# Soft-cap attention and a gated convolution FFN: float64 weights fetched once, six tiles of q and k fetched by rows, a new order

## The chip, the cores and the metric

The kernel runs on one core of a Trainium2 chip. The metric is the device time in microseconds (us) of one execution. Before the change three runs gave 723.64, 722.81 and 723.58 us, the median is 723.58 us. One of them, 723.64 us, was profiled; the rows below come from it. Its span, from the first to the last instruction of the program, is 721.9 us, so 1.7 us lie around it.

## What is computed

Inputs: q, k, v of shape (8 batches, 12 heads, 448, 64) in float32, a cap of 30, and three float64 weights: w_val and w_out (768 x 768) and conv_w (5 x 768).

```python
scores = scale * q @ k.T                      # per batch and head, scale = 1/8
scores = cap * tanh(scores / cap)
attn = exp(scores - max); attn = attn / (sum(attn) + 1e-9)
x = attn @ v                                  # heads side by side: (8, 448, 768)
gate = sigmoid(causal depthwise conv of x with conv_w, 5 taps)
out = (gate * (x @ w_val)) @ w_out            # float32
```

## The kernel before

**Units.** Two heads are one pair, so there are 48 pairs, six for each batch (a block). A pair is held transposed, 128 partitions (2 heads x 64) by 448 positions. Per pair the steps are: load q, k and v; turn q and k (`turn`, L471, VectorE 32x32 block transposes of tiles that `load_blocks` fetched with four DMAs each, in runs of 32 floats); `scores` in four chunks (L501 for three of them, L492 for the last 64 keys); `tanh` and `exp` on ScalarE (L512, L516); `attnv` and `sums` on TensorE (L551); `swap`, a GpSimd memset on which the other half of these products waits (L588); the row sums turned, inverted, moved by four small GpSimd copies (L617, L618) and spread (L623); `mul`; and then the split of x in two float32r parts and five taps of the convolution. `dup` is a GpSimd copy inside the v tile (L769). The first 13 pairs use plain float32 score products, the others three float32r products.

**FFN.** Per block, `val` multiplies x by w_val and `out_part` the gated product by w_out, each in quarters of 18 matmuls (L692). The second quarter of a `val` needs the last three pairs of its block.

**Weights.** [...] `wsteps` cuts the two matrices in twelve parts of 128 x 2 x 384. For each part two DMAs brought the same 768 KB: `weight_load` into `w_raw` as 32-bit words, and `late_load` into `w_late`, placed two bytes further so that the 32 bits in the middle of each float64 are one word. `float64_split` has three steps: first on ScalarE (two passes over the high words, the second in place), second and third on VectorE (2 and 3 instructions). Each scratch tile has one buffer (`RB = 1`).

**Order.** All engines run the order that is written out in three tables, `PAIRS`, `BLOCKS` and `WEIGHTS`: each number is the place of one step, and the steps are issued in ascending order. The engines' queues are in order; SyncE (SP) issues every DMA, so a DMA that waits for a buffer holds those behind it. The numbers are only an order, not times.

**Start.** q and k of pair 0 are loaded before the branch on the cap, into the tiles `u2` that later hold x.

Of the kernel before, what the change touches and what calls it, by code (L numbers as in the profile page):

```python
# [21 lines left out]
P = 128  # L22
# [11 lines left out]
RB = 1  # L34
# [8 lines left out]
    "load_q load_k load_v dup tq tk q_hi k_hi q_lo k_lo scores scores scores scores tanh tanh tanh tanh exp exp exp exp "  # L43
# [4 lines left out]
- - -36.4291 -24.374 -37.9619 -37.5136 - - - - -29.0953 -27.9246 -34.5266 -32.3914 -28.5027 -27.2632 -34.3824 -29.2176  # L48
  -24.6849 -25.7265 -31.13 -28.7197 - - -23.292 -23.2461 -22.7205 -21.0767 -20.9932 -19.802 -18.4009 -17.5513 -17.1655
  -16.0407 -15.7774 -15.7173 -15.1748 -15.0823 -15.0278 -14.5506 -14.1049 -13.877 -13.7921 -12.1034 -11.3551 -8.4558  # L50
  -6.415 -6.392 -6.1725 -5.1224 -4.4352
-37.4386 -37.4387 -35.491 -16.4956 -31.9763 -33.561 - - - - -26.9758 -18.0782 -24.612 -27.4284 -25.6836 -16.3335
  -20.2913 -26.1892 -19.7974 -15.283 -18.6445 -15.7935 - - -14.7101 -13.2839 -12.8874 -12.572 -12.3419 -12.2373
  -12.0247 -11.7255 -10.2241 -9.8171 -9.7551 -9.4464 -9.3257 -9.2797 -8.9784 -8.7292 -8.7165 -8.6069 -8.4916 -7.3936
  -6.0864 -2.8949 -7.1359 -6.0411 -5.329 -5.0552 -3.5349
-37.0301 -36.7637 -10.1568 -8.8454 -19.4908 -17.8612 - - - - -13.7951 -13.7224 -17.7339 -17.092 -13.4291 -11.281
  -13.9097 -14.3472 -9.6416 -10.6643 -11.4185 -12.0276 - - -8.6127 -8.6004 -8.5032 -8.4243 -7.5194 -7.2147 -7.1119
  -6.8708 -6.8368 -6.5822 -6.5821 -6.5008 -6.4379 -6.4378 -6.3814 -6.0863 -5.9744 -5.2517 -4.9229 -4.7084 -3.3457
  -1.1639 -3.9739 -3.7703 -3.5511 -3.4556 -2.9168
# [24 lines left out]
-4.1741 -4.3642 -2.2358 -1.7665 -3.1083 -3.6244 - - - - -2.4685 -1.9312 -1.1375 -2.4014 -2.105 -1.6867 -1.0432 -1.8568
  -1.4142 -1.3686 -0.8526 -0.9598 - - -0.8636 -0.8069 -0.7143 -0.6844 -0.625 -0.5659 -0.4845 -0.4512 -0.3601 -0.326
  -0.251 -0.2504 -0.2414 -0.2063 -0.1205 0.0278 0.3998 0.4886 0.6433 0.7081 1.404 2.5253 1.1579 2.1234 2.7966 2.9888
  3.8991
-5.9312 -3.3656 -1.1405 -0.5559 -2.9017 -2.683 - - - - -0.7716 -1.9644 -1.3399 -1.8509 -0.7511 -1.8327 -1.0977 -1.1584
  -0.5037 -1.3997 -0.0772 -0.0242 0.0805 - -0.0596 0.0005 0.0501 0.0712 0.1653 0.0882 - 0.2485 0.3584 0.4957 0.4993
  0.5303 0.5444 0.5665 - 0.8974 1.0769 1.3554 1.5395 1.561 1.8421 1.9775 2.8868 3.0021 3.8177 3.9114 4.0692  # L90
-2.8216 -3.1447 -1.1298 -0.8483 -2.5982 -1.8133 - - - - -1.2603 -1.5752 -1.3468 -0.9904 -0.6953 -1.5612 -1.0722
  -0.5119 0.4867 0.1382 0.1363 -0.4553 0.7181 - 0.6129 0.6573 0.6654 0.6655 1.0809 0.7518 - 1.081 1.2749 1.4957 1.4958
  1.4959 1.496 1.4961 - 1.6372 1.7452 1.7801 1.8906 1.9143 2.3235 2.5502 2.0327 2.81 3.2719 3.4628 3.5498
-2.2014 -2.8734 -1.1244 1.0266 -1.7634 -1.6803 - - - - -1.5271 -0.8689 -1.1528 0.239 -0.9106 -0.3824 -0.5713 0.388
  1.2563 0.737 1.0745 0.4539 1.6006 - 1.538 1.5604 1.5605 1.5828 1.6328 1.6241 - 1.6329 1.7747 1.9622 1.9713 1.9796
# [146 lines left out]
"""  # L242

WEIGHTS = """
-36.4388 -34.2302 -17.3317 -15.7359 -7.9977
-7.2769 -4.5437 -3.4181 -3.2841 -2.5607
-2.0227 -1.1687 -1.5194 -1.2043 0.239
-0.0716 1.368 1.0934 1.5723 2.0259
# [35 lines left out]
def shifted(t, n):  # L284


    return t.bitcast(I32)[..., 1:2 * n:2]
# [696 lines left out]
```

## Time and profile before

| | |
|---|---|
| median of the runs | 723.58 us |
| the profiled execution | 723.64 us, span 721.9 us |
| TensorE busy | 682.3 us (95%) |
| ScalarE busy | 546.8 us (76%) |
| VectorE busy | 518.9 us (72%) |
| GpSimd busy | 96.5 us (13%) |
| DMA moved | 65.02 MB, 90 GB/s over the span |

PE is TensorE's matmuls, PEld its weight loads, ACT ScalarE, DVE VectorE, POOL GpSimd, SPq the issuing of DMAs. In 40 equal slices of the span (18 us each; a digit is the busy share in tenths) the page shows:

```
PE   4877899799999999999999999999999999999996
DVE  1588798688387676987877966867788785877520
ACT  5888899597787887977877869786989877985311
DMA  6689898866142242325333441225151343110002
```

The chain of work that ended last is 73% TensorE.

### The profile page before, as it was taken

What the parts mean: (1) busy time and instruction counts of PE and PEld (TensorE: products, weight loads), DVE (VectorE), ACT (ScalarE), POOL (GpSimd) and SP (SyncE); (2) the same over time, 40 slices, a digit from 0 to 9 for tenths busy, and PEclk for the clock granted to TensorE, in tenths of its full rate; (3) what the DMA queues carried; (4) which work ended last, traced back from release to release, by engine and by line L of the source; (5) the groups of instructions that cost most, each with busy time, mean ns of one, the idle gap of its engine ahead of it and who ended that gap; (6) DMA issues with size and microseconds to landing.
All of it is one profiled execution on the core that took longest, in us unless ns stands there. A gap on an engine that the chain in (4) does not pass through costs nothing.

```text
span 721.9 us, 30880 instructions
## 1 busy us (share of the span) xinstructions
PE 682.3 (95%) x13714; PEld 577.4 (80%) x13714; DVE 518.9 (72%) x928; ACT 546.8 (76%) x740; POOL 96.5 (13%) x356
## 2 busy tenths in 40 slices
PE   4877899799999999999999999999999999999996
PEld 1554687579989898888888988897888898898995
DVE  1588798688387676987877966867788785877520
ACT  5888899597887787877977869786989877985311
POOL 0111102021002011011102111112111101121000
PEclk9999999899999999999999999999999999999999
DMA  6689898866142242325333441225151343110002
GB/s 125 118 181 205 200 245 181 211 153 117 33 77 63 61 79 54 64 70 104 75 54 67 85 83 33 63 61 115 29 94 36 79 104 56 38 50 25 24 2 92
DMA packets 242284, 65.02 MB, mean 90 GB/s; under 512 B 228832, under 2 KB 236000, under 8 KB 242144
## 3 DMA queue, kind: packets, MB, share of 16 engines
q1 hardware_dynamic: 242144, 62.99, 40.4%
q8 instruction: 109, 1.79, 1.1%
q14 instruction: 31, 0.25, 0.1%
HBM read 51.94 MB, written 11.01 MB: 87 GB/s over the span
## 4 chain that ended last, share of the span: by engine, by line
PE 73%; ACT 3%; DVE 2%; SPq 2%; issue 2%; POOL 0%; DMA 0%; DVEq 0%; POOLq 0%; ACTq 0%
PE psf L692 40%; PE psa L551 19%; PE pss L501 9%; PE pss L692 3%; PE pss L492 2%; SPq L347 1%; ACT pt L512 1%; ACT pt L516 1%; ACT L516 1%; SPq L360 1%; DVE gate L662 0%; ACT g_h L723 0%; DVE g_l L408 0%; DMA vn<-in_v_dram 0%; ACT ph L516 0%
## 5 line engine op out<-in xcount | busy, mean ns | idle before, releaser
L512 ACT ACTIVATE pt<-pss,rc 128x896 f32<-128x896 f32 x144 | 142.8, 1004 | 69.1 <-PE pss L501 67.8
L692 PE MATMUL psf<-wo,g_h 64*128 64x384 f32 x1248 | 163.3, 338 | 1.7 <-POOL token L700 1.6
L692 PE MATMUL psf<-xh,wv 64*128 64x448 f32 x1104 | 161.5, 369 | 1.3 <-ACT xh L646 0.6
L516 ACT ACTIVATE pt<-pt,capt 128x896 f32<-128x896 f32 x144 | 147.0, 1042 | 1.0
L551 PE MATMUL psa<-pt,vn 64*32 64x224 f32 x4416 | 132.3, 355 | 6.7 <-issue 3.5
L662 DVE SCALAR_TENSOR_TENSOR gate<-u,cw,gate 128x448 f32<-128x448 f32 x192 | 126.1, 664 | 2.1 <-ACT gate L658 0.8
L551 PEld LDWEIGHTS psa<-pt,vn 64*32 64x32 f32 x4416 | 80.4, 106 | 51.0 <-issue 23.0
L692 PEld LDWEIGHTS psf<-wo,g_h 64*128 64x128 f32 x1248 | 112.4, 184 | 9.7 <-issue 4.2
L692 PEld LDWEIGHTS psf<-xh,wv 64*128 64x128 f32 x1104 | 103.1, 184 | 15.0 <-issue 3.5
L692 PE MATMUL psf<-wo,g_l 64*128 64x384 f32 x624 | 105.3, 332 | 0.2 <-DVE g_l L408 0.2
L692 PE MATMUL psf<-xl,wv 64*128 64x448 f32 x552 | 102.1, 363 | 0.0
L692 PEld LDWEIGHTS psf<-wo,g_l 64*128 64x128 f32 x624 | 58.9, 184 | 0.6 <-DVE g_l L408 0.5
L692 PEld LDWEIGHTS psf<-xl,wv 64*128 64x128 f32 x552 | 52.6, 184 | 4.7 <-DVE xl L408 0.4
L602 DVE STREAM_TRANSPOSE zt<-psa 128x256 f32<-128x256 f32 x46 | 20.4, 444 | 48.6 <-PE psa L551 48.4
L501 PE MATMUL pss<-qt,kt 64*128 64x448 f32 x156 | 41.4, 622 | 12.1 <-DVE guard L417 8.0
L720 DVE TENSOR_TENSOR gate<-psf,gate 128x448 f32<-128x448 f32 x46 | 27.3, 616 | 34.3 <-PE psf L692 33.2
L623 DVE STREAM_TRANSPOSE zt<-rc 128x512 f32<-128x512 f32 x48 | 34.0, 707 | 24.8 <-POOL rc L618 24.5
L617 POOL COPY rc<-rc 32x8 f32<-32x8 f32 x96 | 34.9, 364 | 122.9 <-DVE rc L610 119.9
L523 DVE TENSOR_TENSOR pa<-pt 128x896 f32<-128x896 f32 x38 | 41.0, 1080 | 13.9 <-ACT pt L516 13.9
L751 ACT COPY osb<-psf 128x384 f32<-128x384 f32 x52 | 23.7, 477 | 32.6 <-PE psf L692 29.8
L723 ACT CAST g_h<-gate 128x448 fp32r<-128x448 f32 x48 | 25.9, 561 | 19.2 <-DVE gate L720 19.2
L501 PE MATMUL pss<-qh,kh 64*128 64x448 f32 x210 | 40.2, 380 | 0.0
(97 smaller groups left out, 1075.4 us busy)
## 6 DMA issues: line engine op xcount, KB each, us to landing
out_dram<-osb SPq DMA_DIRECT2D x56, 192.0 KB, 2.3
kn<-in_k_dram SPq DMA_DIRECT2D x188, 56.0 KB, 2.6
qn<-in_q_dram SPq DMA_DIRECT2D x188, 56.0 KB, 2.7
vn<-in_v_dram SPq DMA_DIRECT2D x96, 96.0 KB, 2.8
w_raw<-in_moe_w_val_dram SPq DMA_DIRECT2D x6, 768.0 KB, 5.4
w_late<-in_moe_w_val_dram SPq DMA_DIRECT2D x6, 768.0 KB, 5.3
w_raw<-in_moe_w_out_dram SPq DMA_DIRECT2D x6, 768.0 KB, 4.9
w_late<-in_moe_w_out_dram SPq DMA_DIRECT2D x6, 768.0 KB, 6.1
```

The costliest lines, as they stand in the source:

```text
L501: nc.tensor.matmul(ps[:, j, :S], st[x][r, c], st[y][r], start=(n == 0), stop=(n == len(parts) - 1))
L512: nc.scalar.activation(st["p", i], st.pop(("s", i)), AF.Tanh, scale=rc8)
L516: nc.scalar.activation(t, t, AF.Exp, scale=capt)
L523: nc.vector.tensor_tensor(st["a"], st["a"] if i else st["p", 0], st["p", i + 1], op=ALU.add)
L551: mm = nc.tensor.matmul(bank(p, h)[o, cols], left, right, start=start, stop=(st["left"][kind] == 0), skip_group_check=True)
L617: nc.gpsimd.tensor_copy(rc[GROUPS[g], 1], rc[GROUPS[g + 1], 1])
L623: nc.vector.transpose(st["zt"][:, :4 * ZQ].rearrange("p (c e) -> p c e", e=BLK), rc)
L662: nc.vector.scalar_tensor_tensor(g, u[:, i:i + S], cw[:, hp, i:i + 1], g, ALU.mult, ALU.add)
L692: mm = nc.tensor.matmul(outs[k], left[r], right[r], start=(swap == 0 and first), stop=(swap == 1 and last))
L720: nc.vector.tensor_tensor(g, psums.pop((b, d))[:, :S], g, op=ALU.mult)
L723: nc.scalar.copy(gated["h"][:, d, TL:], gates[b * NPAIR + d])
L751: nc.scalar.copy(osb, psums.pop((b, "o", m))[:, :NH])
```

## The change

- `weight_load` fetches a part with two DMAs of 128 rows. `late_load` is gone; `low_words` takes its place: a GpSimd copy of the two middle 16-bit words of each float64, 128 x 1536 elements, out of `w_raw`. It reads what the in-place pass of step one overwrites, so that ScalarE pass has to come after it.
- q and k of pairs 0, 1 and 2 (`TURNED = 3`) are fetched by `load_rows`: two DMAs a tile, four rows of 64 floats to a partition. `turns` makes eight TensorE transposes against an identity into one `pss` tile of PSUM, and `tq`, `tk` copy out of PSUM on VectorE. The io tiles and `u2` grow from 448 to 512 columns; GpSimd builds the identity before the branch.
- The three tables are new, with one more step, `turns`. The number of steps of every other kind is as before.

```diff
+def load_rows(nc, t, src, p):
+    _, H, S, D = src.shape
+    b, hp = divmod(p, H // 2)
+    t = t[:CH, :2 * S * D // CH].rearrange("r (n j d) -> r n j d", j=2, d=D)
+    for j in range(2):
+        nc.sync.dma_start(t[:, :, j], src[b, 2 * hp + j].rearrange("(r n) d -> r n d", r=CH))
...
             raw = wsc.tile([P, WC, NH, 2], I32, name="w_raw", bufs=RB)
-            rows = w[c.start * P:c.stop * P, nh * NH:(nh + 1) * NH].bitcast(I32)
-            nc.sync.dma_start(raw.rearrange("p i n t -> p i (n t)"), rows.rearrange("(i p) n -> p i n", p=P))
+            for i in range(WC):
+                r = (c.start + i) * P
+                nc.sync.dma_start(raw[:, i], words(w[r:r + P, nh * NH:(nh + 1) * NH]))
             wstate[n] = raw
-        def late_load(n):
-            w, c, nh, _ = wsteps[n]
-            late = wsc.tile([P, WC, 4 * NH + 2], U16, name="w_late", bufs=RB)
-            rows = w[c.start * P:c.stop * P, nh * NH:(nh + 1) * NH].bitcast(U16)
-            nc.sync.dma_start(late[:, :, 1:1 + 4 * NH], rows.rearrange("(i p) n -> p i n", p=P))
-            wlate[n] = shifted(late, NH)
+        def low_words(n):
+            wlate[n] = wsc.tile([P, WC, NH], I32, name="w_late", bufs=RB)
+            nc.gpsimd.tensor_copy(wlate[n].bitcast(U16).rearrange("p i (n k) -> p i n k", k=2), wstate[n].bitcast(U16)[..., 1:3])
...
+        def turns(p):
+            ps = ps_s.tile([P, 2, 512], F32, name="pss")
+            for x, name in enumerate("qk"):
+                t = loads.pop((name, p))[:CH, :2 * S * D // CH].rearrange("r (n e) -> r n e", e=2 * D)
+                for n in range(S // CH):
+                    nc.tensor.matmul(
+                        ps[:, x, n * CH:(n + 1) * CH], t[:, n], ident[:CH, :CH], start=True, stop=True, is_transpose=True
+                    )
+                loads[name, p] = ps[:, x, :S].rearrange("p (n r) -> p r n", r=CH)
...
-            nc.vector.transpose(t, loads.pop((name, p)))
+            src = loads.pop((name, p))
+            if p < TURNED:
+                nc.vector.tensor_copy(t.rearrange("p (r n) -> p r n", r=CH), src)
+            else:
+                nc.vector.transpose(t, src[:, :S])
```

The first steps of the new order, by queue. SP: k2, weight part 0, k1, q1, the five DMAs of conv_w, v0, v1, q2, part 1, q3. TensorE: `turns` 0, three chunks of scores 0, `turns` 1, the last chunk of scores 0, three chunks of scores 1, `turns` 2, one chunk of scores 1, and then `attnv` 0. ScalarE: two `tanh` of pair 0, step one of weight part 0, a third `tanh`. GpSimd: `low_words` 0, `dup` 0, the small copy of conv_w, `dup` 1, `low_words` 1, `swap` 0. `low_words` is the instruction just ahead of step one, with no other ScalarE step between them, for parts 1, 6, 8, 9 and 11; for part 8 `weight_load`, too, has no ScalarE step between it and step one.

## Rows read from the trace of the kernel before

**Rows 1.** Windows: length, busy us (count) of each engine, clock, DMA share, GB/s

```profile
0.00:180.00 180.00, 151.89 (x3562) 108.53 (x3564) 131.02 (x244) 143.18 (x186) 24.59 (x91) 0.97 0.79 174
180.00:660.00 480.00, 475.50 (x9454) 417.47 (x9452) 367.25 (x649) 390.53 (x530) 69.69 (x253) 1.00 0.32 66
```

**Rows 2.** Waits of TensorE, 0 to 180 us: us in total, times, longest

```profile
PE psa L551 <- issue: 9.7, 6, 3.6
PE pss L501 <- DVE guard L417: 8.0, 1, 8.0
PE pss L492 <- DVE qt L471: 3.1, 2, 1.8
PE pss L501 <- DVE qt L471: 2.7, 3, 1.6
...
PE pss L501 <- issue: 1.0, 1, 1.0
```

**Rows 3.** Windows in which the granted clock (third last column) is lowest

```profile
66.00:72.00 6.00, 4.65 (x56) 2.05 (x64) 5.52 (x11) 4.23 (x7) 1.75 (x5) 0.72 0.72 163
...
131.00:136.00 5.00, 2.03 (x21) 0.89 (x21) 3.63 (x6) 2.12 (x4) 0.09 (x1) 0.66 0.79 141
136.00:144.00 8.00, 8.00 (x140) 5.97 (x140) 3.90 (x9) 3.52 (x5) 0.00 (x0) 0.79 0.86 207
```

**Rows 4.** DMA queues, 130 to 134 us: packets, MB, share of 16 engines

```profile
q1 hardware_dynamic: 2712, 0.59, 84.0%
q8 instruction: 1, 0.02, 2.3%
```

**Rows 5.** DMA issues of the whole span: count, KB each, us to landing

```profile
vn<-in_v_dram SPq DMA_DIRECT2D x96, 96.0 KB, 2.8
...
w_late<-in_moe_w_val_dram SPq DMA_DIRECT2D x6, 768.0 KB, 5.3
```

**Rows 6.** Timeline, 0 to 40 us: start, us, engine, line, operation, count

```profile
6.29 0.40 SPq L439 DMA_DIRECT2D w_raw<-in_moe_w_val_dram  x1
6.74 2.03 SPq L347 DMA_DIRECT2D kn<-in_k_dram  x4
...
11.98 1.01 SPq L360 DMA_DIRECT2D vn<-in_v_dram  x2
13.04 0.73 SPq L361 DMA_DIRECT2D vn<-in_v_dram  x1
...
15.56 0.28 POOL L769 COPY vn<-vn 64x128 f32<-64x128 f32 x1 [10.88 <-DMA vn<-in_v_dram]
...
17.66 1.36 PE L551 MATMUL psa<-pt,vn 64*32 64x224 f32 x48
...
28.72 4.17 SPq L321 DMA_DIRECT2D cw_raw<-in_moe_conv_w_dram  x5
```

**Rows 7.** Timeline, two groups of score matmuls

```profile
15.22 0.61 PE L492 MATMUL pss<-qt,kt 64*32 64x224 f32 x16 [1.36 <-DVE qt L471]
...
20.25 1.02 PE L501 MATMUL pss<-qt,kt 64*128 64x448 f32 x4
```

**Rows 8.** Groups of GpSimd by form: busy us, mean ns, idle before

```profile
L730 POOL TENSOR_SCALAR g_l<-g_l 128x384 fp32r<-128x384 f32 x4 | 2.1, 517 | 1.1 <-DVE g_l L408 1.1
L332 POOL COPY cw_m<-cw_raw 128x60 uint16<-128x60 uint16 x1 | 0.2, 234 | 0.4 <-DMA cw_raw<-in_moe_conv_w_dram 0.4
```

**Rows 9.** Groups of ScalarE by form: busy us, mean ns, idle before

```profile
L668 ACT ACT_TABLE_LOAD x24 | 30.8, 1283 | 0.4
L516 ACT ACT_TABLE_LOAD x23 | 29.5, 1283 | 0.4
...
L300 ACT ACTIVATE w_t<-w_raw 128x768 f32<-128x768 f32 x12 | 11.2, 930 | 1.3 <-DMA w_raw<-in_moe_w_val_dram 0.8 <-DMA w_raw<-in_moe_w_out_dram 0.4
```

**Rows 10.** Timeline around 67 us, VectorE and GpSimd

```profile
66.77 0.18 POOL L617 COPY rc<-rc 32x8 f32<-32x8 f32 x1 [6.21 <-DVE rc L610]
...
67.13 0.58 DVE L408 TENSOR_TENSOR xl<-u,xh 128x448 fp32r<-128x448 f32 x1
67.21 0.55 POOL L617 COPY rc<-rc 32x8 f32<-32x8 f32 x1
```

More of the change, by code (lines that the diff above doesn't have):

```diff
@@ L42 @@
 STEPS = (
-    "load_q load_k load_v dup tq tk q_hi k_hi q_lo k_lo scores scores scores scores tanh tanh tanh tanh exp exp exp exp "
+    "load_q load_k load_v dup turns tq tk q_hi k_hi q_lo k_lo scores scores scores scores tanh tanh tanh tanh exp exp exp exp "
     "add add av av av av sums sums sums sums swap av2 av2 av2 sums2 sums2 sums2 turn_sums recip shift spread mul x_hi x_lo "
@@ new lines @@
+-1.6385 -1.509 -0.1777 0.4865 - -1.6291 -0.6406 - - - - -0.1059 -0.097 0.2865 -0.4254 -0.0041 0.2299 0.5879 -0.3546
+  0.426 0.6017 0.8286 0.8243 - - 0.5078 0.8301 0.9701 0.9702 0.9778 0.9853 1.0253 1.0254 1.1146 1.2279 1.2441 1.3341
+  1.3469 1.3547 1.3909 1.5049 1.5403 1.6201 1.6989 1.7485 2.2673 2.779 2.2192 2.2767 2.2925 2.8204 3.001
+-1.4478 -2.3682 -0.3329 0.5078 - -0.7352 -1.5218 - - - - -0.2547 0.0436 0.057 -0.7006 -0.0982 0.1447 0.3254 -0.0033
+  0.139 0.3565 0.4943 0.5181 - - 0.5762 0.5918 0.6327 0.6414 0.6424 0.6427 0.6686 0.6864 0.6878 0.6884 0.7016 0.7123
+  0.7609 0.9603 1.0221 1.0507 1.0548 1.0989 1.1532 1.1907 2.4555 2.7151 1.4661 2.1357 2.6827 2.933 3.2721
@@ new lines @@
+-1.9115 -2.3483 -0.4141 0.1687 - -0.9563 -1.247 - - - - -0.5341 -0.3823 -0.6029 -0.2015 -0.467 -0.2625 -0.5988 -0.0495
+  -0.2595 0.225 -0.3864 0.2693 - - 0.2757 0.3613 0.3614 0.3615 0.37 0.3701 0.3702 0.3703 0.3935 0.5559 0.556 0.5561
+  0.5992 0.5993 0.5994 0.7161 0.7227 0.7912 1.0268 1.1106 1.9171 2.0192 2.6796 2.9152 2.9406 3.308 3.6016
+-2.2442 -2.5286 -0.5356 -0.5032 - -1.0558 -1.0112 - - - - -0.2888 -0.9159 -0.9622 -0.5875 -0.2095 -0.6062 -0.6227
+  -0.4479 0.0235 -0.2877 -0.2616 -0.2523 - - 0.1587 0.2193 0.2448 0.3779 0.4141 0.5449 0.5788 0.6313 0.639 0.7798
+  0.8115 0.8503 0.8707 0.9729 1.0244 1.0812 1.2195 1.2816 1.3721 1.4335 2.3975 2.5699 1.9494 2.0746 2.2294 3.0315
+  3.1536
@@ new lines @@
+-2.2399 -2.6359 -0.3985 0.67 - -1.227 -0.9804 - - - - -0.8382 -0.029 -0.4885 -0.1912 -0.5516 0.1465 -0.3818 -0.0337
+  0.4745 0.6233 0.4855 0.7528 - - 0.7112 0.9214 0.9277 0.9278 0.9279 0.928 0.9281 0.9282 0.9519 0.9734 0.9735 0.9736
+  0.9737 0.9738 0.9739 1.5419 1.8331 1.8986 1.9946 2.137 2.3625 3.246 2.2122 2.6622 2.7042 3.9978 4.0246
+-2.4046 -1.6476 -0.2473 0.0748 - -0.6617 -1.4629 - - - - -0.2957 -0.5245 0.581 -0.0208 -0.2043 -0.2113 0.6768 0.522
+  0.673 0.2651 1.0378 1.0412 0.8707 - 1.2008 1.2579 1.258 1.2581 1.2583 1.2582 - 1.2584 1.321 1.4874 1.541 1.5839
+  1.584 1.5841 - 1.8854 2.0212 2.0354 2.0355 2.1637 3.5808 3.7577 3.0036 3.072 3.6717 3.8646 4.6128
@@ new lines @@
+-1.2232 -1.4429 1.3692 1.6624 - -0.6145 -0.4235 - - - - 0.1261 -0.2635 -0.0965 0.3196 0.3216 0.013 0.0246 0.5137
+  1.2984 0.5106 0.8566 1.2744 1.6058 - 1.8324 1.8325 1.8326 1.8327 1.8329 1.8328 - 1.833 1.8889 2.1208 2.1209 2.121
+  2.1211 2.1212 - 2.1856 2.1984 2.3689 2.5381 2.5931 2.9586 3.0352 3.2279 3.3001 4.497 4.9183 5.093
+-1.8083 -1.5554 1.1795 1.3277 - -0.6873 -0.6944 - - - - -0.3313 -0.2839 -0.0492 -0.6722 -0.3265 -0.1782 0.4258 -0.4349
+  1.0615 0.1288 0.637 1.5496 1.4166 - 1.6524 1.7421 1.7422 1.7423 1.7513 1.7512 - 1.7514 1.7952 2.4103 2.4104 2.4105
+  2.4396 2.4397 - 2.8091 2.9522 3.0309 3.1033 3.1801 3.9477 4.4556 3.3326 3.6323 3.7025 4.8294 4.8541
@@ L248 @@
--0.0716 1.368 1.0934 1.5723 2.0259
-1.9619 2.3215 2.6778 2.7728 3.1149
-3.1394 3.8865 3.8223 4.1845 4.3555
-4.5604 4.7613 4.5929 4.8031 5.2632
-5.3127 6.3969 5.9147 6.0286 6.6917
-6.9016 6.9528 7.3014 7.4915 7.8789
-8.414 8.6519 8.428 8.7824 8.8246
-9.2527 9.4408 9.4309 9.6281 9.6493
-10.1424 10.2269 10.3277 10.6037 10.8514
-"""
-CW_LOAD, CW_AT, W_FREE = -7.5893, -7.068, 11.4232
+-2.8949 -2.3988 -1.8129 -1.7112 0.1161
+-0.28 0.7322 1.2353 1.7541 1.9238
+2.2053 2.612 2.7193 2.8838 3.3292
+3.0384 3.7192 4.069 4.2197 4.567
@@ L261 @@
+4.4005 4.7567 5.2191 5.2618 5.6827
+5.6503 5.8797 6.0735 6.1981 7.2499
+6.5684 7.3685 7.4088 7.463 7.8574
+7.8228 8.2396 8.3877 8.4024 8.7462
+9.0432 9.0597 9.0732 9.1811 9.5374
+9.2745 9.6296 9.6628 9.9829 9.983
+10.1219 10.39 10.707 10.9262 11.2792
+11.0718 11.5952 11.6438 11.849 11.8491
+"""
+CW_LOAD, CW_AT, W_FREE = -2.0598, -0.5862, 12.1192
+TURNED = 3
 NPAIRED, NPLAIN = 11, 13
@@ L362, in load_v, with fast_path @@
     return vn
-def fast_path(tc, io, u2, q, k, v, w_val, conv_w, w_out, out, capt):
+def fast_path(tc, io, u2, ident, q, k, v, w_val, conv_w, w_out, out, capt):
     nc = tc.nc
@@ L465, in load @@
             if p:
-                loads[name, p] = io.tile([P, S], F32, name=name + "n")
-                load_blocks(nc, loads[name, p], src, p)
+                t = loads[name, p] = io.tile([P, 2 * S * D // CH], F32, name=name + "n")
+                if p < TURNED:
+                    load_rows(nc, t, src, p)
+                else:
+                    load_blocks(nc, t[:, :S], src, p)
+        def turns(p):
[7 more added lines that the diff above has]
+                loads[name, p] = ps[:, x, :S].rearrange("p (n r) -> p r n", r=CH)
         def turn(name, p):
             t = wk.tile([P, S], F32, name=name + "t")
-            nc.vector.transpose(t, loads.pop((name, p)))
+            src = loads.pop((name, p))
+            if p < TURNED:
+                nc.vector.tensor_copy(t.rearrange("p (r n) -> p r n", r=CH), src)
+            else:
+                nc.vector.transpose(t, src[:, :S])
             state.setdefault(p, {})[name] = t
@@ L645, in x_hi @@
             xh = wk.tile([P, S], F32R, name="xh", bufs=NXX)
-            nc.scalar.copy(xh, u2[p % 2][:, PAD:])
+            nc.scalar.copy(xh, u2[p % 2][:, PAD:PAD + S])
             xs[p] = xh
@@ L650, in x_lo @@
             xl = wk.tile([P, S], F32R, name="xl", bufs=NXX)
-            less(nc.vector, xl, u2[p % 2][:, PAD:], xs[p])
+            less(nc.vector, xl, u2[p % 2][:, PAD:PAD + S], xs[p])
             xs[p] = xs[p], xl
@@ L769, in fast_path @@
             dup=lambda p: nc.gpsimd.tensor_copy(vloads[p][D:, :, NK], vloads[p][:P - D, :, NK]),
-            tq=lambda p: turn("q", p), tk=lambda p: turn("k", p),
+            turns=turns, tq=lambda p: turn("q", p), tk=lambda p: turn("k", p),
             q_hi=lambda p: half_hi("q", p), k_hi=lambda p: half_hi("k", p),
@@ L800, in fast_path @@
         for n, row in enumerate(plan(WEIGHTS)):
-            for f, when in zip((weight_load, late_load, weight_first, weight_second, weight_third), row):
+            for f, when in zip((weight_load, low_words, weight_first, weight_second, weight_third), row):
                 at(when, f, n)
@@ L941 @@
         pad = conv_w.shape[0] - 1
-        u2 = [pool.tile([P, pad + q.shape[2]], F32, name=f"u{i}") for i in range(2)]
+        u2 = [pool.tile([P, pad + 2 * q.shape[2] * q.shape[3] // CH], F32, name=f"u{i}") for i in range(2)]
         for t, src in zip(u2, (q, k)):
-            load_blocks(nc, t[:, pad:], src, 0)
+            load_rows(nc, t[:, pad:], src, 0)
+        ident = pool.tile([P, P], F32, name="ident")
+        make_identity(nc, ident)
         mag = pool.tile([1, 1], F32, name="mag")
@@ L950 @@
         with tc.If(flag != 0) as cmp:
-            fast_path(tc, io, u2, q, k, v, w_val, conv_w, w_out, out, capt)
+            fast_path(tc, io, u2, ident, q, k, v, w_val, conv_w, w_out, out, capt)
         with cmp.Else():
```

279 lines of the change are left out of this document (121 added, 158 removed), and 75 rows, old and new, of the table BLOCKS.

## The prediction

> **What bounds the kernel now.** I read the busy table and the slices first, then busy time by stretch, then what TensorE waited for, then the clock, and only then single instructions. From 180 to 660 us TensorE is busy for 475.50 of 480 us [rows 1]. The change takes nothing from that work, so little can be won there. In the first 180 us it is busy for 151.89, which leaves 28.1 us idle, while the DMA share is 0.79 against 0.32 later [rows 1]. This stretch is where the reader must look: the weights arrive in it, the DMA engines are near full, and ScalarE (143.18) and VectorE (131.02) are nearly as busy as TensorE.
>
> The idle time has names [rows 2]. 8.0 us stand before the first score matmul. 5.8 us (3.1 + 2.7) are waits for a turned q, which is late because its loads are late. 10.7 us (9.7 + 1.0) are put to "issue": TensorE stood with nothing that the profile shows to wait for, the longest time 3.6 us. In the four microseconds around that one the ordinary queue held 84.0% of the 16 DMA engines and the queue named "instruction" moved one packet [rows 4]. I read these gaps as instruction blocks that come late behind data. The Trainium skill, "Runtime: NRT & Kernel Launch", Instruction fetch mechanics, says that an engine's instructions are streamed in 16 KiB blocks over a DMA queue of its own, and calls the cost mostly hidden; the queue is there in this trace, and the 3.6 us beside 84.0% speak against "hidden" here. After such pauses the granted clock is 0.72, 0.66 and 0.79 in three windows [rows 3], mixtures of the two levels of 2.4 and 1.2 GHz.
>
> **The change part by part.** The base is the profiled execution: 721.9 span + 1.7 around it = 723.6, which is also the median of the runs (723.58).
>
> *Second fetch of the weights gone.* Twelve transfers of 768 KB leave (six of w_val [rows 5] and six alike of w_out), 9.4 MB of the 31.3 that moved in 180 us (174 GB/s x 180 [rows 1]), so by bytes the DMA share falls from 0.79 to 0.55 (0.79 x 21.9 / 31.3), somewhat less if the small packets of q and k cost more for a byte. Of the 10.7 us of gaps between nothing and all goes; a share of 0.55 lies half way to the 0.32 of the later stretch, where TensorE is idle for only 4.5 of 480 us whatever the reason. I take 7.5. -7.5 (0 to -10.7).
>
> *Clock.* The time at the lower level in these windows [rows 3] is 6 x 0.28 / 0.5 = 3.4, 5 x 0.34 / 0.5 = 3.4 and 8 x 0.21 / 0.5 = 3.4 us. Half of it is lost work, but 3.0 us of the second window were idle anyway, so 1.7 + 0.2 + 1.7 = 3.6. It goes where the pause before it goes. -2 (0 to -3.6).
>
> *Waits for a turned q.* Pairs 1 and 2 come with two DMAs a tile instead of four, later ones wait less behind weights. -3 (0 to -5.8).
>
> *Transposes.* 24 on TensorE. The trace has none. Below stands 0.61 / 16 = 0.04 us for a matmul of 224 columns with a small stationary operand, above 1.02 / 4 = 0.26 for one of 448 columns with 128 stationary ones [rows 7]; a transpose has 112 columns but loads 112 rows of 128, so I take the middle, 0.13. 24 x 0.13 = +3 (1.0 to 6.2). They also hold one of the two score tiles of PSUM until VectorE has copied it out, two copies in place of two transposes, which I cost at nothing. The identity is built while GpSimd waits for the flag: nothing.
>
> *The start.* SP's first issue behind the branch was at 6.29. In the new order k2 (two of the four in 2.03, 1.0), two parts of weight 0 (0.8), k1 and q1 (2.0) bring it to 10.1, the five DMAs of conv_w (4.17) to 14.3, v0 (1.74) to 16.0, v1 to 17.8, q2 to 18.8 [rows 6]. With 2.8 us to landing [rows 5] v0 is there at 18.8 instead of about 15.5, and q2 at 21.6. `turns` 2 needs q2 and stands ahead of `attnv` 0 on TensorE, so that begins after 22 and not at 17.66 [rows 6]: up to 5 us later, and ScalarE's two `tanh` of pair 0 are followed by the weight step, which waits for part 0. Part of it is made up because scores 1 lie before it now. +2.5 (0 to +5).
>
> *GpSimd copies.* Each moves 1536 elements of 16 bits. By bytes it is twice the 0.517 of a 384-element float32 pass (1.0), by elements four times (2.07), by the conv_w copy of 60 elements in 0.234 it is 6.0 [rows 8]. I take 2.0, the element count of the like-sized row. 12 x 2.0 = 24 us lie on an engine that is busy for 24.59 of 180 [rows 1]. Two things make it late. ScalarE's in-place pass must follow the copy, and its first pass takes 0.93 [rows 9]: where both start together ScalarE stands for 1.1, with `tanh` and `exp` queued behind, and TensorE waits for those. Five of the parts have no step between, so 5 x 1.1 = 5.4 on ScalarE, of which I put 1.5 on the path (0 to +5.4; with 6.0 a copy it would be 5 x 5.1 = 25). And `swap` and `dup` queue behind a copy that waits for its DMA.
>
> *Port.* A GpSimd copy of 0.18 took 0.55 beside a two-input VectorE operation of 0.58 [rows 10]: the small copy lost. Whether VectorE loses to a long copy no row shows, so the bounds are 0 and 2.0 for each of twelve. I take +1, since VectorE is idle for 49 of 180 us [rows 1]. The Trainium skill, "SBUF — State Buffer", Who interferes with whom, says that a GpSimd instruction that reads SBUF and a VectorE one with two SBUF inputs exclude each other, and that the second to start is blocked until the first ends. By that rule the whole 24 us could fall on VectorE; the trace [rows 10] agrees with it for the other direction only, and rival C is what it would do here.
>
> *Order.* ScalarE changes table between sigmoid and `exp` 53 times in the new order instead of 47 (24 + 23 [rows 9]), 6 x 1.28 = 7.7 us more. From 180 us on ScalarE is busy for 390.53 of 480 [rows 1], which covers it: 0, or 7.7 if it all fell in the first stretch. Otherwise I counted the steps ahead of the second quarter of the first `val` with their mean durations: the new order has some 5 us more on ScalarE there and 8 more on TensorE, so TensorE has 3 us more to do while it waits for ScalarE. -3 (-6 to +6, the same count twice, either way).
>
> Sum: -7.5 - 2 - 3 + 3 + 2.5 + 1.5 + 1 + 0 - 3 = -7.5. 723.6 - 7.5 = 716.
>
> **Rivals.** *A, more.* All idle time but the first 8.0 goes, 28.1 - 8.0 = 20.1, and the clock's 3.6, against 3 for the transposes: 703. For it: nearly all of it has a DMA in its history. Against: ScalarE is within 9 us of TensorE there (151.89 - 143.18 [rows 1]), so freed time soon meets the next engine.
>
> *B, no change.* The DMA time was cover that nobody needed; the gaps sit at block boundaries whatever the load, and late q becomes late `exp`. Then the transposes' 3 and the start's 2.5 stand against the clock's 2 and the order's 3: 723.6 + 0.5 = 724, or 722 to 725. For it: one instruction block of four microseconds is a thin proof.
>
> *C, slower: the copies.* Each copy holds the VectorE operations behind it for its 2.0 us, or ScalarE's second pass, or a `swap`. 24 us, half of it absorbed in VectorE's idle time, gives 716 + 12 = 728; with long copies 735 or more. It decides from 7.5 / 12 = 0.6 us a copy that reach TensorE. Against: GpSimd's small copies, not VectorE's, were the ones stretched.
>
> *D, slower: a poor start.* The whole 5 us of the start and the table loads (7.7) fall on the path while the gaps remain in part: 723.6 - 4 + 13 = 732 at most, 727 with half of the 13 and a little of the gaps.
>
> *E, it doesn't do what it says.* If the word view makes every 8 bytes a packet, as in the conv_w load, a part of 128 rows of 6 KB becomes 128 such loads of 6 KB, each of which kept SP 0.8 us [rows 6]: over 100 us a part, past 1500 us in all. Unlikely, since both sides are contiguous.
>
> **How the numbers follow.** About 0.2% (1.4 us) is what a measurement here can tell from no change: under 722.1 is faster, over 725.0 slower. Forecast (710 to 721) 0.46, A 0.16, B 0.14, C 0.16, D 0.06, E 0.02. B lies mostly within the bound, 0.12 same and 0.02 faster. Faster 0.46 + 0.16 + 0.02 = 0.64, same 0.12, slower 0.24. The range reaches down into A and up to C's first value: 703 to 728. Alone, the forecast's own range is 710 to 721.
>
> **What would show it.** Right: TensorE's "issue" waits of the first 180 us under 4 us, the DMA share there near 0.6, no clock under 0.8 after 20 us, `attnv` 0 not before 21 us, the copies at 1.5 to 2.5 us each. Wrong: ScalarE or VectorE waiting for `w_late` by GpSimd for more than 6 us in all, VectorE operations beside the copies stretched by 1 us or more, or TensorE idle after 180 us beyond its 4.5 us now.

## The result, and the profile after

The changed kernel takes 714.63 us (median of four runs, 713.13 to 716.47); beside it the kernel before took 723.19 (722.51 to 723.64). The ratio is 0.9884, 95% interval 0.9855 to 0.9912: faster by 8.6 us, where 716 was forecast. The execution profiled after took 715.56 us, its span is 713.7. One execution each of two kernels below took 1694 and 1322 us, far off the others, and stands in no ratio.

First the stretches (columns as in [rows 1]), the kernel after:

```profile
0.00:180.00 180.00, 159.74 (x3672) 117.80 (x3680) 137.62 (x244) 149.41 (x194) 45.97 (x106) 1.00 0.58 122
180.00:660.00 480.00, 478.32 (x9586) 416.80 (x9572) 375.33 (x658) 395.10 (x535) 64.43 (x253) 1.00 0.32 66
660.00:713.70 53.70, 46.87 (x499) 44.29 (x496) 15.20 (x28) 8.81 (x18) 2.26 (x11) 0.97 0.10 36
```

Take TensorE's idle time, length minus the first busy figure. In the first 180 us it falls from 28.1 [rows 1] to 20.3, in the next 480 from 4.5 to 1.7, and at the end it hardly moves (7.0 to 6.8). TensorE's busy time in all rises from 682.3 to 684.9. So -7.8 - 2.8 - 0.2 + 2.6 = -8.2, the difference of the spans. The DMA share of the first stretch is 0.58 and not 0.79. VectorE and ScalarE are busy for longer there (137.62 and 149.41 us): the stretch holds more of the kernel, and 6.7 us of VectorE's are operations that a copy holds up (below).

The waits of TensorE in that stretch, after; they answer to [rows 2]:

```profile
PE psa L569 <- issue: 6.5, 7, 1.7
PE pss L478 <- DMA u<-in_q_dram: 5.3, 1, 5.3
PE psf L569 <- issue: 1.9, 2, 1.3
...
PE pss L519 <- ACT w_t L293: 1.3, 1, 1.3
PE pss L519 <- DVE qt L487: 1.2, 1, 1.2
PE pss L478 <- DMA qn<-in_q_dram: 1.1, 1, 1.1
...
PE pss L510 <- DVE qt L489: 0.3, 1, 0.3
```

Read them in three lots. The wait before the first product, 8.0 before, is now 5.3 and 0.2 for the DMAs of q and k and 1.2 for the copied q of pair 0. The waits for later q, 5.8 before, are 1.1 + 0.3 = 1.4. The "issue" time is 6.5 + 1.9 = 8.4 against 10.7: shorter, but not gone, and its longest gap is 1.7 and not 3.6. Two of its nine gaps are of another kind. There the products of a pair wait until VectorE's `mul` has read the PSUM tile `psa` that they overwrite:

```profile
68.67 0.62 DVE L658 TENSOR_TENSOR u<-psa,zt 128x448 f32<-128x448 f32 x1
...
69.40 1.37 PE L569 MATMUL psa<-pt,vn 64*32 64x224 f32 x48 [0.79 <-issue]
```

`mul` ends at 69.30 and the products start 0.1 us later; the other gap of 0.65, at 79.88, is the same. Without these two 7.0 us of "issue" remain, and all of the 10.7 before.

The start of TensorE, after (columns as in [rows 6]):

```profile
5.35 0.98 PE L478 MATMUL pss<-ident,u 112*128 112x112 f32 x4 [5.35 <-DMA u<-in_q_dram]
...
16.31 3.36 PE L519 MATMUL pss<-qt,kt 64*128 64x448 f32 x8
...
19.62 1.00 PE L510 MATMUL pss<-qt,kt 64*32 64x224 f32 x16
...
22.13 0.57 PE L478 MATMUL pss<-ident,qn 112*128 112x112 f32 x4
...
24.39 1.37 PE L569 MATMUL psa<-pt,vn 64*32 64x224 f32 x48
```

Four transposes take 0.98 us at first and 0.57 later. The same sixteen score matmuls that took 0.61 at 15.22 before [rows 7] still take 1.00 at 19.62 here: TensorE stays at the lower of its two rates until 20.8 us, where before it had left it by 15.22. The clock's column says 1.00 here, but the trace has no record of the clock before 20.76 us (before the change: 13.12), so the rate is read from durations. The eight score matmuls at 16.31 take 3.36 us, as long as at a granted clock of 0.50 in the run with another start (below):

```profile
16.62 3.36 PE L520 MATMUL pss<-qt,kt 64*128 64x448 f32 x8 [2.74 <-ACT pt L531]
```

Behind the start the kernel before fell to the lower level twice; the execution profiled after does not until its last 4 us:

```profile
67.75:71.15 3.40, 3.40 (x19) 1.18 (x8) 2.99 (x5) 3.00 (x5) 0.85 (x3) 0.50 0.66 144
132.60:139.40 6.80, 5.43 (x93) 2.83 (x101) 2.52 (x4) 2.55 (x4) 0.09 (x1) 0.50 0.88 239
```

`attnv` 0 starts at 24.39, against 17.66 [rows 6]. `mul` 0 then ends at 36.0 instead of 28.5 us, but `mul` 5 at 79.8 instead of 83.0 and `mul` 11 at 168.4 instead of 173.8. The delay is made up within six pairs.

The GpSimd copy and VectorE's convolution taps of the first 170 us, after, as tiles (count, then least, median and greatest ns, first and last start):

```profile
L447 POOL COPY w_late<-w_raw x12: 1464/1464/1897, 11.9 to 144.4; 128x1536 uint16<-128x1536 uint16 x12
L680 DVE SCALAR_TENSOR_TENSOR gate<-u,cw,gate x42: 594/678/1907, 37.0 to 168.9; 128x448 f32<-128x448 f32 x42
```

ScalarE's waits for the copy in the first 180 us, after:

```profile
ACT w_raw L294 <- POOL w_late L447: 2.5, 3, 1.3
```

And one place in the timeline after where copy and taps meet:

```profile
46.81 3.10 DVE L680 SCALAR_TENSOR_TENSOR gate<-u,cw,gate 128x448 f32<-128x448 f32 x3
47.37 1.46 POOL L447 COPY w_late<-w_raw 128x1536 uint16<-128x1536 uint16 x1 [3.11 <-DMA w_raw<-in_moe_w_val_dram]
```

The taps of the kernel before:

```profile
L662 DVE SCALAR_TENSOR_TENSOR gate<-u,cw,gate x39: 592/678/704, 39.3 to 166.1; 128x448 f32<-128x448 f32 x39
```

The medians of the taps agree, 678 and 678; only the greatest differs. Seven of the 42 taps after take 1.08 to 1.91 us, 11.4 us together where seven at the median take 4.7, and each of the seven overlaps a copy. At 46.81 three taps take 3.10, not 2.03, while the copy runs its undisturbed 1.46. So a copy holds the tap, a VectorE operation with two inputs, that meets it, 6.7 us in all.

The Trainium skill, "SBUF — State Buffer", "SBUF: two separate sides", calls the shared port pair an exclusive lock that the first to start keeps for its whole instruction. The trace agrees, in both directions: 1.91 us for a held tap, and 1.90 for a held copy.

### The profile page after: what moved, and what is told of

It is laid out like the page before. It is cut to its first block, busy times and chain, and to the rows that moved or that the text cites. A ratio compares the mean times of both kernels' runs of the same rounds, so it can differ in the third digit from the quotient of the medians.

```text
span 713.7 us, 30968 instructions
## 1 busy us (share of the span) xinstructions
PE 684.9 (96%) x13738; PEld 578.9 (81%) x13738; DVE 528.1 (74%) x928; ACT 553.3 (78%) x746; POOL 112.7 (16%) x370
## 3 DMA queue, kind: packets, MB, share of 16 engines
q8 instruction: 109, 1.79, 1.1%
## 4 chain that ended last, share of the span: by engine, by line
PE 75%; DVE 2%; ACT 1%; issue 1%; DMA 1%; POOL 0%; SPq 0%; POOLq 0%; ACTq 0%; DVEq 0%
PE psf L710 42%; PE psa L569 19%; PE pss L519 10%; PE pss L710 3%; PE pss L510 2%; DVE pa L541 1%; DMA kn<-in_k_dram 1%; ACT pt L530 0%; ACT pt L534 0%; POOL rc L636 0%; DVE u L658 0%; DVE zt L641 0%; ACT L534 0%; ACT g_h L741 0%; DVE wo L298 0%
## 5 line engine op out<-in xcount | busy, mean ns | idle before, releaser
L680 DVE SCALAR_TENSOR_TENSOR gate<-u,cw,gate 128x448 f32<-128x448 f32 x192 | 133.8, 706 | 2.5 <-ACT gate L676 1.1
L569 PE MATMUL psa<-pt,vn 64*32 64x224 f32 x4416 | 129.4, 353 | 5.0 <-issue 3.6
L710 PEld LDWEIGHTS psf<-wo,g_h 64*128 64x128 f32 x1248 | 113.9, 184 | 8.4 <-issue 5.1
L710 PEld LDWEIGHTS psf<-wo,g_l 64*128 64x128 f32 x624 | 60.4, 184 | 0.0
L530 ACT ACTIVATE ph<-pss,rc 128x448 f32<-128x448 f32 x48 | 30.1, 631 | 28.1 <-PE pss L510 27.0
L635 POOL COPY rc<-rc 32x8 f32<-32x8 f32 x96 | 29.9, 312 | 107.8 <-DVE rc L628 104.6
L541 DVE TENSOR_TENSOR pa<-pa,pt 128x896 f32<-128x896 f32 x35 | 38.0, 1086 | 8.3 <-ACT pt L534 7.5
L519 PE MATMUL pss<-qt,kt 64*128 64x448 f32 x156 | 39.9, 609 | 3.9 <-ACT pt L530 1.3
```

What stands on the lines that cost most here:

```text
L519: nc.tensor.matmul(ps[:, j, :S], st[x][r, c], st[y][r], start=(n == 0), stop=(n == len(parts) - 1))
L530: nc.scalar.activation(st["p", i], st.pop(("s", i)), AF.Tanh, scale=rc8)
L541: nc.vector.tensor_tensor(st["a"], st["a"] if i else st["p", 0], st["p", i + 1], op=ALU.add)
L569: mm = nc.tensor.matmul(bank(p, h)[o, cols], left, right, start=start, stop=(st["left"][kind] == 0), skip_group_check=True)
L635: nc.gpsimd.tensor_copy(rc[GROUPS[g], 1], rc[GROUPS[g + 1], 1])
L680: nc.vector.scalar_tensor_tensor(g, u[:, i:i + S], cw[:, hp, i:i + 1], g, ALU.mult, ALU.add)
```

## The experiments

Three groups ran, each group on one chip with the kernel before beside it (medians 720.81, 719.91 and 719.82 us). The theory: the gain is the DMA load of the second fetch, which leaves; row fetch, order and copies are worth little each. The rivals: the new order, or the row fetch, gives the gain; or the copies eat a large part of a gain that would be greater.

**The new order alone**: the second fetch back, at the place of the copy, and tiles by blocks. A part is still fetched by two DMAs.

```diff
-TURNED = 3
+TURNED = 0
-            nc.gpsimd.tensor_copy(wlate[n]...)
+            nc.sync.dma_start(late[:, :, 1:1 + 4 * NH], rows.rearrange("(i p) n -> p i n", p=P))
...
-                if when is not None:
+                if when is not None and name != "turns":
```

> The new order alone: the second fetch of the weights is back at the place of the copy, and no tile is fetched by rows (no transposes on TensorE). Theory (the DMA load is what costs): DMA share of the first 180 us back near 0.75, TensorE's issue waits there 10 us or more, time 719 to 723. Rival (the order brings the gain): 713 to 716, with issue waits that don't matter.

Measured 723.01 us, ratio 1.0030 (1.0007 to 1.0052). The first windows of this kernel:

```profile
0.00:180.00 180.00, 149.83 (x3482) 108.16 (x3490) 127.72 (x236) 140.71 (x182) 27.30 (x89) 0.96 0.76 171
180.00:660.00 480.00, 478.24 (x9539) 417.62 (x9525) 373.99 (x657) 400.75 (x540) 65.55 (x254) 1.00 0.32 67
```

and waits of TensorE in the first 180 us:

```profile
PE psa L572 <- issue: 5.4, 5, 2.1
PE pss L522 <- DVE qt L492: 4.5, 1, 4.5
...
PE pss L513 <- issue: 2.0, 3, 1.0
PE psf L572 <- issue: 1.9, 2, 1.5
...
PE psf L713 <- issue: 0.7, 1, 0.7
```

With the share back at 0.76 the late q (4.5) and the issue time (10.0, of which 2.1 behind a `mul`) are back, and the clock's mean is 0.96. The order by itself is worth nothing, rather a little less. It does shorten TensorE's idle time after 180 us, to 1.8 from 4.5 [rows 1], and loses as much ahead of it.

**Fetched once, in the old order**: the three tables as before, tiles by blocks, no transposes; the copy stands just ahead of step one. Against the kernel before, besides `weight_load` and `low_words` as in the change:

```diff
-            for f, when in zip((weight_load, late_load, weight_first, ...
+            row[1] = min(row[1], row[2] - 0.0001)
+            for f, when in zip((weight_load, low_words, weight_first, ...
```

> The old order with the weights fetched once: the GpSimd copy in place of the second fetch, just ahead of the step that overwrites. Theory (the DMA load costs): 715 to 719, no window with a granted clock under 0.8 after 20 us. Rival (the order brings the gain, or the copies eat it): 721 to 727.

Measured 713.4 us, ratio 0.9898 (0.9875 to 0.9921), which can't be told from the whole change. It is under the 715 to 719 that were expected, and against expectation the clock is at the lower level once, from 65.6 to 69.0. Its first stretch has a share of 0.58 and 4.9 us of issue time, 1.5 of them behind a `mul`; waits for later q are 5.8 as before. Its windows:

```profile
0.00:180.00 180.00, 156.87 (x3636) 114.71 (x3638) 137.60 (x244) 150.08 (x196) 43.43 (x104) 0.99 0.58 122
180.00:660.00 480.00, 476.17 (x9592) 418.37 (x9590) 373.75 (x661) 384.88 (x524) 71.89 (x257) 1.00 0.32 66
```

and its waits of TensorE:

```profile
PE psa L549 <- issue: 4.6, 4, 1.5
PE pss L499 <- DVE qt L469: 3.0, 3, 1.8
PE pss L490 <- DVE qt L469: 2.8, 2, 1.8
```

**The whole change without row fetch and transposes.**

```diff
-TURNED = 3
+TURNED = 0
...
-            load_rows(nc, t[:, pad:], src, 0)
+            load_blocks(nc, t[:, pad:pad + q.shape[2]], src, 0)
```

> The changed kernel without the row fetches and transposes (all of q and k by blocks, turned on VectorE). Theory: the 3 us of transposes and the 3 us of shorter waits cancel, 713 to 717. Rival (the row fetch carries the gain): 719 to 723, with waits of 4 us or more for a turned q in the first 180 us.

Measured 712.11 us, ratio 0.9882 (0.9857 to 0.9907), not to be told from the change with them, and just under the 713 expected. The waits for later q and k are 4.5 us here (3.0 + 1.2 + 0.3) and 1.4 with the row fetch; against that stand the transposes' own 5 us, where the prediction had 3 and 3. On this chip it is also the other side of the new order alone: 712.11 against 723.01, 10.9 us, and but for the widths of some tiles and an unused identity the two differ only in the second fetch or the copy in its place.

**The whole change, with the same rows fetched once more** into a buffer in DRAM that nobody reads. It brings the load back, and no wait for it.

```diff
+            idle = idles.tile([WC, P, 2 * NH], I32, name="w_idle")
             for i in range(WC):
                 r = (c.start + i) * P
+                nc.sync.dma_start(idle[i], w[r:r + P, nh * NH:(nh + 1) * NH].bitcast(I32))
```

> The changed kernel with the 9.4 MB put back as a load that nobody waits for: beside each weight part the same rows are fetched again, to DRAM. Theory: instruction blocks and q come late again, issue waits from 8.4 to 12 us or more, time 718 to 722. Rival (DMA time is cover that nobody needs): 713 to 716.

Measured 724.03 us, ratio 1.0040 (1.0014 to 1.0066), over the 718 to 722 expected. Windows of this kernel, the last two where the granted clock (third last column) is low:

```profile
0.00:180.00 180.00, 152.59 (x3464) 110.11 (x3466) 132.67 (x235) 139.04 (x179) 45.49 (x103) 0.96 0.69 171
180.00:660.00 480.00, 478.61 (x9561) 418.06 (x9560) 374.59 (x658) 400.67 (x543) 63.42 (x252) 1.00 0.32 67
...
32.95:36.35 3.40, 3.40 (x70) 1.76 (x74) 1.67 (x3) 2.61 (x4) 0.00 (x0) 0.50 0.85 193
108.00:112.00 4.00, 4.00 (x22) 3.03 (x24) 2.84 (x6) 2.37 (x3) 2.81 (x5) 0.57 0.59 116
```

and its waits of TensorE in the first 180 us:

```profile
PE psa L574 <- issue: 8.5, 7, 3.1
...
PE psf L574 <- issue: 3.5, 2, 1.8
PE pss L483 <- DMA qn<-in_q_dram: 3.4, 1, 3.4
PE pss L515 <- issue: 1.7, 1, 1.7
```

This is the decisive run: the program that computes is the same, and its whole gain is gone. Issue time goes from 8.4 to 13.7 us, the wait for q from 1.1 to 3.4, and the lower clock level comes back in two places, at 33 and at 108 us. Of the 9.8 us by which the span grows, 5.9 are issue gaps that do not stand behind a `mul` (12.9 against 7.0), 2.3 the wait for q, and 2.7 longer busy time of TensorE (684.9 to 687.6); the rest, -1.1, is scattered. `mul` 11 ends at 179.5 instead of 168.4; what follows 180 us is as in the kernel after (478.61 of 480). The load, not a wait for a weight, is what the second fetch cost. 24 more issues in SP's queue, 16.4 us of its time, belong to it, and for the wait for q the run doesn't part them from the bytes; the issue gaps end behind packets of another queue (last section).

**The copies**, doubled, and left out (the middle words come from a tile of zeros, so the low parts of the weights are missing):

```diff
+            for _ in range(2):
+                nc.gpsimd.tensor_copy(wlate[n]..., wstate[n]...)
```

```diff
-            nc.gpsimd.tensor_copy(wlate[n]..., wstate[n]...)
+            if not wlate:
+                wlate["all"] = wsc.tile([P, WC, NH], I32, name="w_late", bufs=1)
+                nc.gpsimd.memset(wlate["all"], 0)
```

> The changed kernel with each of the twelve GpSimd copies made twice, the second over the first: 12 x 1.46 = 17.5 us more on GpSimd, and ScalarE's in-place pass waits for it. By the terms of the prediction (1.5 + 1 us for copies of 2.0, on the path through ScalarE and VectorE) 1 to 3 us over the changed kernel. Rival (GpSimd's copies hold VectorE or a swap): 6 us or more. Rival (all of it is hidden): within 1 us.

> The changed kernel without the copies: the middle words are read from one tile of zeros, so the low parts of the weights are missing. Theory (the copies cost little): 0 to 2.5 us under the changed kernel. Rival (they cost what doubling them would): 5 us or more under it.

The changed kernel ran beside them:

> The changed kernel as it is, beside the three that follow, on their chip. Both theories: 0.986 to 0.991 of the kernel before.

Measured 713.24 us for the change (0.9893, 0.9863 to 0.9923), 721.19 doubled (1.0021, 1.0002 to 1.0039) and 710.06 left out (0.9861, 0.9827 to 0.9894). The interval without copies overlaps that of the change, so its 3 us are a middle value and not a proof; that of the doubled copies lies far off, so their 8 us stand: not the theory's 1 to 3, but the rival's 6 or more. Left out, they give a little more than the 2.5 that the theory allowed. ScalarE's wait for the doubled copies:

```profile
ACT w_raw L294 <- POOL w_late L448: 9.3, 6, 2.3
```

the taps:

```profile
L681 DVE SCALAR_TENSOR_TENSOR gate<-u,cw,gate x41: 592/680/1883, 36.8 to 168.9; 128x448 f32<-128x448 f32 x41
```

and three windows of that kernel:

```profile
15.70:22.50 6.80, 5.33 (x28) 1.89 (x28) 4.91 (x12) 6.11 (x10) 1.12 (x3) 0.50 0.68 172
66.90:70.30 3.40, 3.40 (x12) 2.03 (x12) 3.33 (x8) 3.40 (x6) 1.60 (x5) 0.50 0.62 118
138.60:142.00 3.40, 3.40 (x20) 2.87 (x18) 3.40 (x3) 3.40 (x6) 3.19 (x2) 0.50 0.37 58
```

ScalarE waits 6.8 us longer for copies. Twelve VectorE operations with two inputs are held and not seven (nine taps and three `g_l`), and five with one input too, 14.8 us in all. The clock's lower level is back in the second and third window; in the first the changed kernel was at the lower rate as well, until 20.8. Beside the change on its chip the span is 7.9 us longer, and 4.0 of these are longer busy time of TensorE (684.1 to 688.1). So about half of what a second copy costs is longer busy time, most of it at the lower rate, and the other half is waiting. Which of the pauses brings the clock down I did not isolate.

**A start in which `attnv` 0 should come earlier**: k and q of pair 1 fetched first, conv_w later.

```diff
-CW_LOAD, CW_AT, W_FREE = -2.0598, -0.5862, 12.1192
+CW_LOAD, CW_AT, W_FREE = 1.37, 2.54, 12.1192
+MOVED = {("load_k", 1): -3.0566, ("load_q", 1): -3.0566, ("load_k", 2): -0.75}
```

> The changed kernel with another start: k and q of pair 1 ahead of the first weight part, k of pair 2 after the two v, the conv_w DMAs and their steps later (behind q of pair 3, before the first tap). By the prediction's term for the start (2.5 us, up to 5): first product with v at 19 to 22 us instead of 24.4, 1 to 4 us under the changed kernel. Rival (ScalarE is the limit there and v was not late): within 1 us of it, although the first product comes earlier.

Measured 715.79 us, ratio 0.9935 (0.9911 to 0.9958), on the chip where the change had 0.9893: no better, by the middle values 2.6 us worse. `attnv` 0 starts at 24.95, no earlier than 24.39, and the clock, in the execution profiled:

```profile
15.90:22.70 6.80, 5.89 (x28) 1.90 (x28) 3.73 (x6) 5.64 (x7) 1.00 (x1) 0.50 0.85 171
43.20:50.00 6.80, 5.62 (x119) 3.33 (x116) 6.39 (x11) 4.89 (x7) 2.33 (x6) 0.50 0.66 162
104.60:108.00 3.40, 3.40 (x16) 2.42 (x16) 1.90 (x5) 1.97 (x3) 1.35 (x4) 0.50 0.03 7
```

So this did not test what an earlier start is worth: it did not bring one. What it lost is the clock: the second and third window are 10 us at the lower level that the change does not have, and TensorE's busy time is 688.4 us against 684.1 on the same chip. Whether the shift of the loads brings them or the single execution does is not shown.

**Where the copy should run**: on ScalarE, on VectorE, or on GpSimd in four pieces of 384 elements.

```diff
-            nc.gpsimd.tensor_copy(wlate[n]..., wstate[n]...)
+            nc.scalar.copy(wlate[n]..., wstate[n]...)
```

(or `nc.vector.tensor_copy` in the same place), and the pieces:

```diff
+            for i in range(0, NH, NH // 4):
+                nc.gpsimd.tensor_copy(late[:, :, i:i + NH // 4], ...)
```

> The twelve copies of middle words on ScalarE instead of GpSimd, all else as changed. Theory (a GpSimd copy costs because VectorE's two-input operations run beside it at 833 instead of 666 ns, some 7 us of VectorE in the first 170 us, of which 2 to 3 reach the end): the taps go back to a mean of 670 ns over that stretch, but ScalarE, busy for 149 of 180 us, takes 12 x 1.5 = 18 us more and becomes the bound there: 716 to 722. Rival (the copy's own length in the chain load, copy, second pass is what costs, not the port): ScalarE's waits of 2.5 us go, nothing else changes much, and the time is 710 to 713 if ScalarE still has room.

> The twelve copies on VectorE instead of GpSimd. Theory (port): the taps go back to 670 ns, which gives VectorE some 7 us back in the first 170 us; the copies cost it 12 x 0.8 to 1.6 = 10 to 19 us, so VectorE loses 3 to 12 us in all and the time is 713 to 718. Rival (no port; the stretched taps have another cause): taps stay at 800 ns or more and VectorE is busy for 160 of 180 us, over 720.

> Each GpSimd copy cut into four of 384 elements by the columns. Theory (VectorE is held while one GpSimd copy runs): a held operation waits for 0.4 us and not for up to 1.5, but the sum of the copies is a little longer (four times an issue cost of about 0.1 us, so 1.8 to 2.0 us a part), and the total of VectorE in 0 to 180 us stays within 3 us of the 149: 712 to 716, no difference that can be measured. Rival (a tap costs the rest of one copy, once a copy): three quarters of the stretch goes, taps near 710 ns, 710 to 712.

Measured 719.52 us on ScalarE (0.9991, 0.9967 to 1.0016), 714.72 on VectorE (0.9933, 0.9905 to 0.9960), 712.18 in pieces (0.9899, 0.9869 to 0.9929). Copies and taps of the one on ScalarE:

```profile
L447 ACT COPY w_late<-w_raw x12: 1454/1462/1487, 12.3 to 153.6; 128x1536 uint16<-128x1536 uint16 x12
L680 DVE SCALAR_TENSOR_TENSOR gate<-u,cw,gate x41: 593/678/687, 38.4 to 167.6; 128x448 f32<-128x448 f32 x41
```

of the one on VectorE:

```profile
L447 DVE COPY w_late<-w_raw x12: 917/953/1045, 11.9 to 146.7; 128x1536 uint16<-128x1536 uint16 x12
L680 DVE SCALAR_TENSOR_TENSOR gate<-u,cw,gate x41: 593/677/700, 36.8 to 162.2; 128x448 f32<-128x448 f32 x41
```

and of the pieces:

```profile
L449 POOL COPY w_late<-w_raw x48: 497/505/972, 11.7 to 146.2; 128x384 uint16<-128x384 uint16 x48
L682 DVE SCALAR_TENSOR_TENSOR gate<-u,cw,gate x42: 591/678/1016, 37.3 to 168.3; 128x448 f32<-128x448 f32 x42
```

Off GpSimd no tap is longer than 0.70 us: the long taps are the copy's doing and nothing else's. On ScalarE the twelve copies, 17.6 us, eat the whole gain, as the theory of a near-full ScalarE said. On VectorE the copy is the shortest (0.95) and the time lies between. In pieces the longest tap falls from 1.91 to 1.02, but four pieces take 2.0 us and not 1.46, and the time is that of the change (0.9893), as the theory had it. No version here beats the change by more than its interval.

## Why the prediction was right

The time was right within 2 us. Its terms, one by one:

- **Second fetch, -7.5 by shorter issue gaps: the step that was mis-sized.** The share came out at 0.58, as worked out (0.55), but the gaps did not shrink with it to 3 us: 8.4 stayed, 7.0 of them of the kind that was meant, so -3.7 (and +1.4 for the new waits behind `mul`). That is one execution: at shares of 0.56 to 0.60 the nine other traces have 0.7 to 7.3. The rest of the saving came from the same cause in other places, the waits for q and the clock. All of it together, taken alone in the old order, is -1.0% or 7.4 us; in the new order it is 10.9 us (723.01 against 712.11).
- **Clock, -2.** All the time at the lower level between 20.8 us and the end region is gone. TensorE was busy for 8.8 of its 10.2 us, so it is worth 4.4, past the bound of 3.6, which had put 3.0 idle us into it. Against it stands the start, where TensorE works at its lower rate for 12.6 us and not 4.9: 3.8 lost, 1.9 of them in transposes, which count below, and 1.9 in scores. The sum had no such term.
- **Waits for q, -3:** -4.4 (5.8 to 1.4). **Transposes, +3:** six groups of four measured 0.98, 0.98, 0.98, 0.95, 0.57 and 0.55, 5.0 us, since four of them ran at the lower rate; at the upper rate 0.14 each, against the 0.13 taken. Both together are near nothing (+0.6), as forecast.
- **Start, +2.5.** `attnv` 0 came 6.7 us later, past the 5 at most, but it is made up by `mul` 5. The price on the path was not isolated.
- **Copies, +1.5 + 1.** 1.46 us each, not 2.0; ScalarE waited for 2.5 us. VectorE lost 6.7 us to the port, so rival C's mechanism is there, and by the prediction's own sign (operations stretched by 1 us or more) it was wrong to price it by small copies alone. But left out, the copies give back about 3 us, near the 2.5; that VectorE's idle time took the rest is likely and not shown. C's 12 on the path did not come; twice the copies cost 11.1 (721.19 against 710.06).
- **Order, -3 (-6 to +6):** alone it is +0.3%, beside the single fetch 712.11 against 713.4, which is not clear of noise. It shows in another place than the first `val`: after 180 us TensorE is idle for 4.5 and 3.8 us in the two traces of the old order, and for 1.4 to 1.8 in the eleven of the new one.
- **Rivals.** A did not come: 20.3 us of idle time stayed in the first stretch, where it left 8.0. Nor did D's 727 to 732. B is ruled out by the repeated fetch, which returns to 724. Its remark that the gaps sit at block boundaries whatever the load is half right (below). E is out: the words came in packets of 3072 bytes.

So the sum was near because errors met. By the executions profiled, the parts are: gaps -3.7, waits behind `mul` +1.4, later q -4.4, transposes +5.0, clock -4.4, lower rate of the start +1.9, first product -1.3, after 180 us -3.0, other waits +0.1; that is -8.4, and the spans differ by -8.2. Too much was put to the gaps (3.8), 2 too little to the transposes, and nothing to the waits behind `mul`. Against that the later q gave 1.4 more, the wait for the first product 1.3, and of the 5 us charged to start and copies little shows in TensorE's waits (1.3 for `w_t`), though some of it is the start's lower rate. Of the signs that the prediction named, the "issue" time under 4 us failed, and VectorE operations stretched by 1 us or more, a sign of being wrong, were there.

## What to carry to other kernels

Traffic that nobody waits for can still cost: here 9.4 MB behind 0.79 of the DMA engines were worth 1 to 1.5%, through late operands, late instructions and the lower clock that followed some of the pauses. To see whether a fetch costs by its load or by its wait, fetch the same bytes once more for nobody. When work goes to an idle engine, look for what that engine shares: the median of VectorE's taps hides it, the greatest shows it.

## What the runs showed of the hardware

Every gap of TensorE over 0.3 us that the profile puts to "issue" and that doesn't stand behind a `mul` is at one kind of place. Counted in all of TensorE's instructions from the start of the program (matmuls, weight loads, and its own waits and branches), the gaps before open behind numbers 705, 1473, 2497, 3009, 4289, 5313, 6081 and 16577, after behind 449, 1729, 3009, 3521, 4289, 5569 and 6081: each is 193 plus a multiple of 256, and so it is in all thirteen kept traces. The queue of kind "instruction" moves packets of 16 KB (109 for 1.79 MB, before and after alike), and each of the fourteen gaps among them in the first 180 us ends 1.2 to 2.0 us after one such packet has ended. So the gaps are instruction blocks that come late.

The load bears on how late, but does not set it alone. In the first 180 us these gaps are 10.7 us before, 8.0 with the new order alone and 12.9 with the rows fetched once more, at shares of 0.69 to 0.79; at 0.56 to 0.60 they are 7.0 in the changed kernel and 0.7 to 7.3 in the nine others, the 0.7 without the row fetch. What TensorE has to do counts as well: the 256 instructions ahead of each of the seven gaps after took it only 2.9 to 4.0 us. Four other blocks went as fast without a gap; their packets had ended 1.1 to 1.9 us after TensorE passed the place 256 instructions earlier, those of the seven 2.1 to 3.4 us after it.

The Trainium skill, "Runtime: NRT & Kernel Launch", Instruction fetch mechanics, gives such blocks as 16 KiB or 256 instructions and the cost of a crossing as mostly hidden. The spacing agrees; most of the crossings are hidden here as well (seven of some thirty show in the first 180 us after), but those that are not cost up to 12.9 us in kernels of 720.
